# Moving small steps between the engines of a tuned attention and mixture-of-experts kernel: GpSimd scales one group, weights are asked for later, and the next attention's first scores sit inside the expert's output

## The chip, the cores and the metric

The kernel runs on one core of a Trainium2 chip. The metric is the device time in microseconds of one launch. Before the change it is 382.05 us, the median of three runs (381.8 to 382.43). The profile is of one such execution; its span, from the first to the last instruction, is 380.1 us.

The engines are named as in the profile: PE is the matrix engine (PEld its weight loads), DVE the vector engine, ACT the scalar engine, POOL is GpSimd, and SP the sync engine, which here only issues DMA transfers.

## The reference, cut to what matters

There are 8 batches of 384 tokens. Each batch goes through an attention with 16 query heads on 4 key and value heads, and the result, 384 x 1024, is the input x of a mixture of experts with 4 groups of 4 experts.

```python
# attention, per batch
scores = scale * np.matmul(q, k.transpose(0, 1, 3, 2))
attn = softmax(scores)
x = np.matmul(attn, v)                       # heads side by side: [B*S, 1024]
# mixture of experts, per token
g_idx = argmax(x @ w_group);  g_w = softmax weight of that group
e_idx = argmax(x @ w_expert[g_idx]);  e_w = softmax weight of that expert
h  = np.maximum(x @ w1[g, e], 0.0)
out = g_w * e_w * (h @ w2[g, e])
```

## The kernel before

An attention (`Attn`) runs in 24 units: 4 groups (one key head with its 4 query heads) of 6 key chunks. A unit makes scores on PE, takes exp on ACT into a tile `e` in SBUF, multiplies `e` with v on PE into the group's accumulator `oT` in PSUM, and lets POOL and DVE sum the `e` tiles for the softmax's denominator.

```python
def score(self, u):
    sT = ps_tile("s")                        # PSUM, two buffers in turn
    ... 4 matmuls ...                        # L305
    e = epool.tile([P, 2, S], F32, name="e") # 13 buffers
    nc.scalar.activation(e, sT, ACT.Exp, scale=scale)            # L311

def pv(self, u):
    if c == 0:
        self.oT[g] = ps_tile("o")            # PSUM, two buffers in turn
    ... 4 matmuls, oT[g] += v * e[u] ...     # L324

def tail(self, u):
    if c in (1, 3):
        self.add(nc.gpsimd, u - 1)           # L331: e[u-1] += e[u]
    if c >= 3:
        self.reduce(g, c - 3, ...)           # L338, DVE (can be held back)
    if c == NC - 1:
        self.reduce(g, NR - 1, z + 2)
        ...
        if b > 2 or (b == 2 and g > 1):
            nc.vector.tensor_copy(out=dst, in_=src)              # L371, oT -> xT
        else:
            nc.scalar.copy(out=dst, in_=src)                     # L373

def run(self, u0, u1, inserts, nxt=None):
    for u in range(u0, u1):
        if u + 2 < NU: self.score(u + 2)
        elif nxt is not None: nxt.score(u + 2 - NU)
        self.pv(u)
        self.tail(u)
        for f in inserts.get(u, []): f()     # other work, placed after unit u
```

`ps_tile("x")` gives the "o" buffer of PSUM that is not in turn; inserts use it. After the attention the sums of the denominators are gathered (`collect`, DVE), spread over partitions by a small matmul (`sums`, L405) and inverted (L409). For each pair of the eight column blocks (`m`), `spread` writes the inverses out with DVE transposes into `rb` (L416), `scale_x` multiplies `xT` by them (L425), and `cast` makes the bf16 copy `xb` that the expert reads.

The expert of a batch is guessed from the mean of v before its tokens are known, so that its weights can be fetched ahead; what a guess gets wrong is done in a loop at the end. `guess_mean` (L457) and `guess_logits` (L473) make the guess, `gate_logits` (L443) and `gate_tokens` (L468) the logits of the tokens, `gate_softmax` and `pick_index` are some 14 small DVE operations, and `pick`, `pick_w1` (L544) and `pick_w2` (L550) read the index on POOL and start the two weight transfers of 2048 KB each.

The first two batches are woven by hand:

```python
a = at[0]
a.run(0, NU, {
    ...
    9: [do(first_k, 1, "x", nc.vector)],
    10: [do(sums, 0, 0, 1, "x"), do(normalise, 0, 0)],
    13: [first_guess],
    15: [do(collect, 0, 1, 2), first_pick],
    16: [first_fetch],                       # pick, pick_w1(0)
    19: [do(sums, 0, 1, 2, "x")],
    20: [do(normalise, 0, 1)],
    21: [do(pick_w2, 0)],
}, at[1])
collect(0, 2, Hkv)
loads(2)                                     # v, k and q of batch 2
a = at[1]
hold(a)
a.run(0, FU, {                               # FU = 15
    2: [do(cast, 0, 0)],
    4: [do(cast, 0, 1)],
    7: [do(sums, 0, 2, Hkv, "x")],
    8: [do(normalise, 0, 2, "x"), do(normalise, 0, 3, "x"), a.release, do(transposes, 2)],
    11: [do(cast, 0, 2)],
    13: [do(cast, 0, 3)],
})
moe_h(0, 0, "s")                             # expert 0, first half (L606, L608)
...
a.run(FU, NU, {})
```

From batch 2 on every batch is the same block: an attention, then the expert of the batch before it. The end of the expert's output (`ffn_y`, L615) for its third chunk of tokens, and the start of the next attention:

```python
y = ffn_y(w2s[f], hTs[f], 2, "o", (0,))      # first half of the columns
guess_logits(vm, glp)
at[b + 1] = Attn(b + 1)
at[b + 1].score(0)
weights[b] = gate_softmax(b, glp, not last)
pick_index(b + 1)
ffn_y(w2s[f], hTs[f], 2, "o", (1,), y)       # second half
at[b + 1].score(1)
return {1: [do(y_out, f, 2, y, True)]}       # half on ACT, half on DVE, after unit 1
```

Of the kernel before, what the change touches and what calls it, by code (L numbers as in the profile page):

```python
# [9 lines left out]
F32 = mybir.dt.float32  # L10
# [3 lines left out]
ALU = mybir.AluOpType  # L14
# [4 lines left out]
def kernel(  # L19
# [218 lines left out]
    def evac(eng, out_, in_):  # L238
        if eng is nc.scalar:
            eng.copy(out=out_, in_=in_)  # L240
        else:
            eng.tensor_copy(out=out_, in_=in_)  # L242
# [46 lines left out]
    class Attn:  # L289
# [62 lines left out]
        def tail(self, u):  # L352
            b = self.b
            g, c = u // NC, u % NC
            z = u - c
            if c in (1, 3):
                self.add(nc.gpsimd, u - 1)
            if c >= 3:
                self.reduce(g, c - 3, (z, z + 4, z + 5)[c - 3])
            if c == NC - 1:  # L360
                self.reduce(g, NR - 1, z + 2)
                if b not in xT:
                    if b == 1:
                        w = wpool.tile([P, KQ, F], BF16, name="w1")
                        xT[b] = w.rearrange("p a f -> p (a f)").bitcast(F32)[
                            :, :KQ * S].rearrange("p (a n) -> p a n", n=S)
                    else:
                        xT[b] = xpool.tile([P, KQ, S], F32, name="xT", bufs=1)
                dst, src = xT[b][:, KG * g:KG * (g + 1), :], self.oT[g][:, :, :S]
                if b > 2 or (b == 2 and g > 1):  # L370
                    nc.vector.tensor_copy(out=dst, in_=src)  # L371
                else:
                    nc.scalar.copy(out=dst, in_=src)  # L373
# [37 lines left out]

    def spread(b, m, which=None):

        rb = gpool.tile([P, 2, S], F32, name="rb") if which is None else ps_tile(which)[:, :, :S]
# [12 lines left out]
    def normalise(b, m, which=None):  # L427
        scale_x(b, m, spread(b, m, which), nc.vector)

    def cast(b, m):  # L430
        ks = slice(2 * m, 2 * m + 2)
        nc.scalar.copy(out=xb[b][:, ks, :], in_=xT[b][:, ks, :])  # L432

# [13 lines left out]
        nc.scalar.copy(out=ls, in_=lg[:, :S])  # L447
        lgs[b] = ls

    def guess_mean(b, pt, eng=None):  # L450

        pm = pt[:, 1, :Hkv]
        v16 = vraw[b].rearrange("p h x -> p (h x)").bitcast(BF16)
        for g in range(Hkv):
            for i in range(SC):
                e0 = g * NC * D + i * P
                nc.tensor.matmul(out=pm[:, g:g + 1], lhsT=v16[:, 2 * e0 + 1:2 * (e0 + P):2],  # L457
                                 rhs=onesb[:, :1], start=(i == 0), stop=(i == SC - 1))
        vm = gpool.tile([P, Hkv], BF16, name="vm")
        evac(eng or nc.vector, vm, pm)  # L460
        return vm

    def gate_rows(pt):
# [146 lines left out]
    def ffn_y(w2, hT, c, which, nhs=(0, 1), y=None):  # L610
        if y is None:
            y = ps_tile(which)
        for nh in nhs:
            for f in range(FQ):
                nc.tensor.matmul(out=y[:, nh, :], lhsT=hT[:, f, c * P:(c + 1) * P],  # L615
                                 rhs=w2[:, f, nh * HALF:(nh + 1) * HALF],
                                 start=(f == 0), stop=(f == FQ - 1))
        return y

    hTs = {}  # L620

# [5 lines left out]
    def y_out(b, c, y, split=False):  # L627
        ot = opool.tile([P, DM], F32, name="ot")
        if split:
            nc.scalar.mul(ot[:, :HALF], y[:, 0, :], weff[b][:, c:c + 1])  # L630
            nc.vector.tensor_scalar(ot[:, HALF:], y[:, 1, :], weff[b][:, c:c + 1], None,  # L631
                                    op0=ALU.mult)
        else:
            nc.scalar.mul(ot, y.rearrange("p a n -> p (a n)"), weff[b][:, c:c + 1])  # L634
        for ps, x in halves(c):
            nc.sync.dma_start(out=out_rows(out[b * S:(b + 1) * S])[x], in_=ot[ps])

# [3 lines left out]
    def do(f, *a):  # L641
        return lambda: f(*a)
# [21 lines left out]

    def first_guess():
        state["pt"] = ps_tile("x")
        state["vm"] = guess_mean(0, state["pt"], nc.scalar)

    def first_pick():
        glp = gate_rows(state["pt"])  # L670
# [19 lines left out]
    def hold(a):  # L690
        a.held = []

    GB = KG * SC
    a = at[0]
    a.run(0, NU, {
# [2 lines left out]
        4: [gate_matrix_b],  # L698
        6: [do(collect, 0, 0, 1)],
        7: [do(first_q, 2 * GB, 2 * GB, "x", nc.vector)],  # L700
        9: [do(first_k, 1, "x", nc.vector)],
        10: [do(sums, 0, 0, 1, "x"), do(normalise, 0, 0)],
        13: [first_guess],
        15: [do(collect, 0, 1, 2), first_pick],
        16: [first_fetch],
        19: [do(sums, 0, 1, 2, "x")],
        20: [do(normalise, 0, 1)],
        21: [do(pick_w2, 0)],
    }, at[1])
    collect(0, 2, Hkv)  # L710
    loads(2)

    FU = 15
    a = at[1]
    hold(a)
    a.run(0, FU, {
        2: [do(cast, 0, 0)],
        4: [do(cast, 0, 1)],
        7: [do(sums, 0, 2, Hkv, "x")],
        8: [do(normalise, 0, 2, "x"), do(normalise, 0, 3, "x"), a.release, do(transposes, 2)],  # L720
        11: [do(cast, 0, 2)],
        13: [do(cast, 0, 3)],
    })
    moe_h(0, 0, "s")
    pt = ps_tile("x")
    gate_logits(0, pt)
    moe_h(0, 2, "s")
    glp = gate_rows(pt)
    gate_tokens(0, glp)
    vm = guess_mean(1, pt, nc.scalar)  # L730
    collect(1, 0, 2)
    sums(1, 0, 2, "s")
    for m in range(2):
        normalise(1, m)
    moe_h(0, 4, "s")
    guess_logits(vm, glp)
    weights[0] = gate_softmax(0, glp, True, nc.scalar)
# [5 lines left out]
    def first_block():  # L743

        prefetch(1)
        collect(1, 2, Hkv)
        weights[0]()
        out_weights(0)
        cast(1, 0)
        cast(1, 1)  # L750
        moe_y(0, 0, "s")
        y = ffn_y(w2s[0], hTs[0], 1, "s", (0,))
        sums(1, 2, Hkv, "o")
        normalise(1, 2)
        normalise(1, 3)
        ffn_y(w2s[0], hTs[0], 1, "s", (1,), y)
        y_out(0, 1, y)
        cast(1, 2)
        cast(1, 3)
        nc.sync.dma_start(out=xb_dram[1], in_=xb[1])  # L760
        y = ffn_y(w2s[0], hTs[0], 2, "o", (0,))
        at[2] = Attn(2)
        at[2].score(0)
        ffn_y(w2s[0], hTs[0], 2, "o", (1,), y)
        at[2].score(1)
        return {1: [do(y_out, 0, 2, y, True)], 3: [second_logits], 19: [second_gate],
                21: [second_pick]}

    def second_logits():
        gate_logits(1, ps_tile("x"))  # L770

    def second_gate():
        state["pt"] = ps_tile("x")
        gate_tokens(1, gate_rows(state["pt"]))
        state["vm"] = guess_mean(2, state["pt"])

    def second_pick():
        glp = gate_rows(state["pt"])
        guess_logits(state["vm"], glp)
        weights[1] = gate_softmax(1, glp, True, nc.scalar)  # L780
        pick_index(2)

    def prefetch(b):
# [8 lines left out]
    def block(b):  # L792
        last = b == B - 1
        f = b - 1
        prefetch(b)
        moe_h(f, 0, "s")
        collect(b, 0, Hkv)
        weights[f]()
        out_weights(f)
        moe_h(f, 2, "s")  # L800
        sums(b, 0, Hkv, "o")
        for m in range(4):
            normalise(b, m)
# [12 lines left out]
        pt = ps_tile("s")  # L816
        glp = gate_rows(pt)
        gate_tokens(b, glp)
        vm = None if last else guess_mean(b + 1, pt)
        y = ffn_y(w2s[f], hTs[f], 2, "o", (0,))  # L820
        if not last:
            guess_logits(vm, glp)
            at[b + 1] = Attn(b + 1)
            at[b + 1].score(0)
        weights[b] = gate_softmax(b, glp, not last)
        if not last:
            pick_index(b + 1)
        ffn_y(w2s[f], hTs[f], 2, "o", (1,), y)
        if not last:
            at[b + 1].score(1)  # L830
            return {1: [do(y_out, f, 2, y, True)]}
        y_out(f, 2, y, True)
        weights[b]()
        out_weights(b)

# [119 lines left out]
```

The softmax here doesn't subtract the row's maximum and nothing guards it: scores larger than these inputs give would overflow.

## Time and profile before

| | before |
|---|---|
| time, median of 3 | 382.05 us |
| span of the profiled execution | 380.1 us |
| PE busy | 364.6 us, 96% |
| DVE busy | 261.9 us, 69% |
| ACT busy | 232.6 us, 61% |
| POOL busy | 147.3 us, 39% |
| granted PE clock | 0.996 |

PE busy is the union of its matmuls' time, so what is left, 15.5 us, is the time in which no matmul was under way. The chain that ended last runs through PE for 78% of the span, DVE for 13% and ACT for 6%. Where it leaves PE, another engine kept PE waiting. These places lie in the first two attentions, at the start of the third, and for about four microseconds at the start of each later one.

### The profile page before, as it was taken

Reading aid. Unit: us, or ns where it says so; the run is one execution under the profiler, and the core shown is the slowest. Engines: PE = TensorE matmul, PEld = TensorE weight load, DVE = VectorE, ACT = ScalarE, POOL = GpSimd, SP = SyncE. Lnnn points to the kernel's source line nnn. Section 1 sums busy time; section 2 is a strip of 40 time slices with the busy share of each in tenths; the row PEclk is TensorE's granted clock in tenths of the full one; section 3 lists DMA queues with packets and bytes.
Section 4 is the critical chain, followed back from the end, with each engine's and each line's share of the span. In section 5 each row is a group of like instructions: output and inputs, shape, how many; then the busy total and the mean of one; then the engine's idle time right before and its main releaser. Section 6 shows DMA issues by size and latency. Waiting matters only on the chain.

```text
span 380.1 us, 8950 instructions
## 1 busy us (share of the span) xinstructions
PE 364.6 (96%) x3663; PEld 193.9 (51%) x3663; DVE 261.9 (69%) x494; ACT 232.6 (61%) x315; POOL 147.3 (39%) x116
## 2 busy tenths in 40 slices
PE   8999799999989999999999999999999999999992
PEld 3444356444545455545555455554555456554541
DVE  4789978847689279854998279883798449983130
ACT  4779945768824498256953489344982569544321
POOL 5657730716613077212653047330772036600000
PEclk9999999999999999999999999999999999999998
DMA  8975999999999999899999999999998999199734
GB/s 190 247 115 93 238 211 149 241 237 260 207 160 223 252 248 184 173 211 297 213 148 221 228 278 208 148 220 254 244 185 163 182 282 228 30 207 220 236 68 100
DMA packets 71209, 76.02 MB, mean 200 GB/s; under 512 B 35928, under 2 KB 50264, under 8 KB 71168
## 3 DMA queue, kind: packets, MB, share of 16 engines
q0 software_dynamic: 26640, 41.03, 61.8%
q1 hardware_dynamic: 44096, 33.81, 36.1%
q10 hardware_dynamic: 432, 0.61, 0.5%
q8 instruction: 29, 0.48, 0.5%
q14 instruction: 12, 0.10, 0.1%
HBM read 89.21 MB, written 18.87 MB: 284 GB/s over the span
## 4 chain that ended last, share of the span: by engine, by line
PE 78%; DVE 13%; ACT 6%; issue 2%; ACTq 0%; DVEq 0%; POOLq 0%
PE ps_o L324 22%; PE ps_s L606 18%; PE ps_s L615 14%; PE ps_o L615 7%; PE ps_s L305 7%; ACT e L311 4%; DVE red L338 4%; PE ps_o L443 3%; DVE xT L425 2%; DVE rb L416 2%; PE ps_o L268 1%; PE ps_o L606 1%; DVE w L425 1%; PE ps_s L468 1%; PE ps_o L405 1%
## 5 line engine op out<-in xcount | busy, mean ns | idle before, releaser
L331 POOL TENSOR_TENSOR e<-e 128x768 f32<-128x768 f32 x64 | 116.1, 1830 | 138.5 <-ACT e L311 91.5
L311 ACT ACTIVATE e<-ps_s 128x768 f32<-128x768 f32 x192 | 149.1, 819 | 25.2 <-PE ps_s L305 23.5
L324 PE MATMUL ps_o<-e,v_raw 64*64 64x384 f32 x1536 | 153.8, 482 | 1.6 <-DVE xT L425 1.6
L338 DVE TRANSPOSE_TENSOR_REDUCE red<-e 128x24 f32<-128x768 f32 x128 | 114.1, 946 | 10.5 <-POOL e L331 10.5
L606 PE MATMUL ps_s<-xb,w 128*128 128x384 bf16 x480 | 81.0, 326 | 0.0
L324 PEld LDWEIGHTS ps_o<-e,v_raw 64*64 64x64 f32 x1536 | 61.0, 133 | 28.5 <-issue 20.0
L305 PE MATMUL ps_s<-qT,kT 64*64 64x384 bf16 x768 | 67.1, 327 | 3.0 <-ACT e L311 1.7
L608 ACT ACTIVATE hT<-ps_s 128x768 bf16<-128x768 f32 x30 | 24.3, 811 | 70.9 <-PE ps_s L606 70.9
L606 PEld LDWEIGHTS <-w 128*128 128x128 bf16 x512 | 48.8, 98 | 36.3 <-issue 4.8
L615 PEld LDWEIGHTS <-hT 128*128 128x128 bf16 x384 | 36.0, 98 | 45.4 <-issue 5.4
L615 PE MATMUL ps_s<-w,hT 128*128 128x512 bf16 x248 | 56.4, 379 | 0.0
L305 PEld LDWEIGHTS <-kT 64*64 64x64 bf16 x768 | 29.4, 104 | 42.6 <-issue 39.1
L615 PE MATMUL ps_o<-w,hT 128*128 128x512 bf16 x136 | 32.0, 379 | 0.0
L416 DVE STREAM_TRANSPOSE rb<-inv 128x384 f32<-128x384 f32 x60 | 31.1, 557 | 1.0
L425 DVE TENSOR_TENSOR xT<-xT,rb 128x768 f32<-128x768 f32 x26 | 28.2, 1086 | 0.9
L634 ACT ACTIVATE ot<-ps_s,we 128x1024 f32<-128x1024 f32 x14 | 15.6, 1116 | 19.1 <-PE ps_s L615 19.1
L432 ACT CAST xb<-xT 128x768 bf16<-128x768 f32 x28 | 22.1, 832 | 0.0
L371 DVE COPY xT<-ps_o 128x768 f32<-128x768 f32 x22 | 20.2, 919 | 0.0
L242 DVE CAST vm<-ps_s 128x4 bf16<-128x4 f32 x5 | 0.8, 163 | 27.4 <-PE ps_s L457 27.4
L663 POOL COPY after<-qT 128x1 bf16<-128x1 bf16 x7 | 1.3, 189 | 40.5 <-DMA qT<-q_raw 37.5
L631 DVE TENSOR_SCALAR ot<-ps_o,we 128x512 f32<-128x512 f32 x7 | 5.3, 750 | 15.6 <-ACT ot L630 11.3
L409 DVE RECIPROCAL inv<-ps_o 128x96 f32<-128x96 f32 (+2 forms) x10 | 6.0, 603 | 7.0 <-PE ps_o L405 7.0
(129 smaller groups left out, 189.3 us busy)
## 6 DMA issues: line engine op xcount, KB each, us to landing
w<-in_moe_w_dram POOLq DMA_DIRECT2D x16, 2048.0 KB, 21.9
out_dram<-ot SPq DMA_DIRECT2D x42, 256.0 KB, 7.0
xb_scratch<-xb SPq DMA_DIRECT2D x8, 768.0 KB, 9.8
q_raw<-in_q_dram POOLq DMA_DIRECT2D x7, 768.0 KB, 33.6
v_raw<-in_v_dram SPq DMA_DIRECT2D x14, 384.0 KB, 7.3
out_dram<-ot SPq DMA_DIRECT2D x11, 128.0 KB, 2.3
k<-in_k_dram POOLq DMA_DIRECT2D x7, 192.0 KB, 30.3
w<-in_q_dram POOLq DMA_DIRECT2D x3, 192.0 KB, 7.3
```

The lines of the kernel that those rows point to most:

```text
L305: nc.tensor.matmul(out=sT[r * H2:(r + 1) * H2, s, :S], lhsT=kT[b][s * D:(s + 1) * D, slot, ks], rhs=qT[b][s * D:(s + 1) * D, kq * SC:(kq + ...
L311: nc.scalar.activation(e.rearrange("p t (s x) -> p s t x", s=2), sT[:, :, :S].rearrange("p s (t x) -> p s t x", t=2), ACT.Exp, scale=scale)
L324: nc.tensor.matmul(out=oT[t * D:(t + 1) * D, r, :S], lhsT=vraw[b][r * H2:(r + 1) * H2, g, c * D:(c + 1) * D], rhs=self.e[u][r * H2:(r + 1) ...
L331: eng.tensor_add(out=self.e[u], in0=self.e[u], in1=self.e[u + 1])
L338: nc.vector.tensor_reduce(out=reds[self.b][:, g, n].rearrange("p t j -> p (t j)"), in_=self.e[u].rearrange("p t (j x) -> p (t j) x", x=32) ...
L371: nc.vector.tensor_copy(out=dst, in_=src)
L416: nc.vector.transpose(out=rb[:, r].rearrange("p (j x) -> p j x", x=32), in_=inv[b][:, 2 * m + r].unsqueeze(2).to_broadcast([P, NB, 32]))
L425: eng.tensor_mul(out=x, in0=x, in1=rb)
L432: nc.scalar.copy(out=xb[b][:, ks, :], in_=xT[b][:, ks, :])
L606: nc.tensor.matmul(out=h[:, jj, :S], lhsT=w1[:, kq, (f0 + jj) * P:(f0 + jj + 1) * P], rhs=x[:, kq, :], start=(kq == 0), stop=(kq == KQ - 1))
L608: nc.scalar.activation(hT[:, f0:f0 + 2, :], h[:, :, :S], ACT.Relu)
L615: nc.tensor.matmul(out=y[:, nh, :], lhsT=hT[:, f, c * P:(c + 1) * P], rhs=w2[:, f, nh * HALF:(nh + 1) * HALF], start=(f == 0), stop=(f == ...
```

## The change

The change moves steps; the arithmetic stays, and nothing is left out.

- In the first attentions GpSimd takes over the multiplication and the bf16 copy of batch 0's group 1, and the multiplication of batch 1's first two groups; the copy of group 0 moves ahead into attention 0. Keys are transposed one unit earlier. The sums of batch 0's groups 2 and 3 come three units earlier, their normalisation two units earlier, and the held reductions are released three units later. This is to take work from DVE and ACT while both have more than PE.
- The second weights of expert 0 and the loads of batch 2 are asked for later, so that the first weights have the transfers to themselves; DVE takes the `xT` copies of batch 1's group 1 and of batch 2's first two groups.
- Batch 1's logits and its gate come out of attention 2's units 3, 19 and 21: the logits into the expert's output before it, the gate to unit 2.
- Both first scores of an attention sit inside the second half of the expert's last output chunk, three of whose eight steps come before them and five after, and the whole chunk is then written by DVE. This is to have the first two exps done by the time the attention begins.

The diff, cut:

```diff
-                if b > 2 or (b == 2 and g > 1):
+                if b > 1 or (b, g) == (1, 1):
                     nc.vector.tensor_copy(out=dst, in_=src)
...
-        rb = gpool.tile([P, 2, S], F32, name="rb") if which is None else ...
+        rb = gpool.tile([P, 2, S], F32, name="rb", bufs=2) if which is None else ...
...
-    def cast(b, m):
+    def cast(b, m, eng=None):
         ks = slice(2 * m, 2 * m + 2)
-        nc.scalar.copy(out=xb[b][:, ks, :], in_=xT[b][:, ks, :])
+        evac(eng or nc.scalar, xb[b][:, ks, :], xT[b][:, ks, :])
...
+    def y_scores(f, a, y):
+        ffn_y(w2s[f], hTs[f], 2, "o", (1,), y, range(FQ // 2 - 1))
+        a.start()                            # score(0), score(1)
+        ffn_y(w2s[f], hTs[f], 2, "o", (1,), y, range(FQ // 2 - 1, FQ))
+        y_out(f, 2, y, nc.vector)
...
+    def first_scale():
+        scale_x(0, 1, state["rb"], nc.gpsimd)
+        cast(0, 1, nc.gpsimd)
+    def first_spread():
+        state["rb"] = spread(0, 1)
...                                          # attention 0
-        9: [do(first_k, 1, "x", nc.vector)],
+        8: [do(first_k, 1, "x", nc.vector)],
...
+        14: [do(cast, 0, 0)],
...
-        20: [do(normalise, 0, 1)],
-        21: [do(pick_w2, 0)],
+        20: [first_spread],
+        21: [first_scale],
     }, at[1])
     collect(0, 2, Hkv)
-    loads(2)
...                                          # attention 1
-        2: [do(cast, 0, 0)],
-        4: [do(cast, 0, 1)],
-        7: [do(sums, 0, 2, Hkv, "x")],
-        8: [do(normalise, 0, 2, "x"), do(normalise, 0, 3, "x"), a.release, do(transposes, 2)],
-        11: [do(cast, 0, 2)],
+        3: [do(pick_w2, 0)],
+        4: [do(sums, 0, 2, Hkv, "x")],
+        6: [do(normalise, 0, 2, "x"), do(normalise, 0, 3, "x")],
+        9: [do(load_k, 2), do(load_q, 2)],
+        10: [do(cast, 0, 2)],
+        11: [a.release],
         13: [do(cast, 0, 3)],
     })
     moe_h(0, 0, "s")
+    load_v(2)
+    transposes(2)
...
     for m in range(2):
-        normalise(1, m)
+        scale_x(1, m, spread(1, m), nc.gpsimd)
...                                          # the expert's output before attention 2
         y = ffn_y(w2s[0], hTs[0], 2, "o", (0,))
+        gt = ps_tile("x")
+        guess_mean(2, gt)
+        gate_logits(1, gt)
+        state["vm"] = mean_copy(gt, nc.vector)
         at[2] = Attn(2)
-        at[2].score(0)
-        ffn_y(w2s[0], hTs[0], 2, "o", (1,), y)
-        at[2].score(1)
-        return {1: [do(y_out, 0, 2, y, True)], 3: [second_logits], 19: [second_gate],
-                21: [second_pick]}
+        y_scores(0, at[2], y)
+        return {2: [second_gate]}
...                                          # the later blocks
         if not last:
             guess_logits(vm, glp)
-            at[b + 1] = Attn(b + 1)
-            at[b + 1].score(0)
         weights[b] = gate_softmax(b, glp, not last)
         if not last:
             pick_index(b + 1)
+            at[b + 1] = Attn(b + 1)
+            y_scores(f, at[b + 1], y)
+            return {}
         ffn_y(w2s[f], hTs[f], 2, "o", (1,), y)
-        if not last:
-            at[b + 1].score(1)
-            return {1: [do(y_out, f, 2, y, True)]}
-        y_out(f, 2, y, True)
+        y_out(f, 2, y, nc.vector)
```

More of the change, by code (lines that the diff above doesn't have):

```diff
@@ L412, in spread @@
     def spread(b, m, which=None):
-        rb = gpool.tile([P, 2, S], F32, name="rb") if which is None else ps_tile(which)[:, :, :S]
+        rb = gpool.tile([P, 2, S], F32, name="rb", bufs=2) if which is None else ps_tile(which)[:, :, :S]
         for r in range(2):
@@ L448, in gate_logits, with guess_mean @@
         lgs[b] = ls
-    def guess_mean(b, pt, eng=None):
+    def guess_mean(b, pt):
         pm = pt[:, 1, :Hkv]
@@ L458, in guess_mean, with mean_copy @@
                                  rhs=onesb[:, :1], start=(i == 0), stop=(i == SC - 1))
+    def mean_copy(pt, eng):
         vm = gpool.tile([P, Hkv], BF16, name="vm")
-        evac(eng or nc.vector, vm, pm)
+        evac(eng, vm, pt[:, 1, :Hkv])
         return vm
@@ L608, in ffn_h, with ffn_y @@
         nc.scalar.activation(hT[:, f0:f0 + 2, :], h[:, :, :S], ACT.Relu)
-    def ffn_y(w2, hT, c, which, nhs=(0, 1), y=None):
+    def ffn_y(w2, hT, c, which, nhs=(0, 1), y=None, fs=None):
         if y is None:
@@ L613, in ffn_y @@
         for nh in nhs:
-            for f in range(FQ):
+            for f in (range(FQ) if fs is None else fs):
                 nc.tensor.matmul(out=y[:, nh, :], lhsT=hT[:, f, c * P:(c + 1) * P],
@@ L625, in moe_h, with y_out @@
         ffn_h(xb[b], w1s[b], hTs[b], f0, which)
-    def y_out(b, c, y, split=False):
+    def y_out(b, c, y, eng=None):
         ot = opool.tile([P, DM], F32, name="ot")
[L629 to L632, printed above, removed]
+        w = weff[b][:, c:c + 1]
+        if eng is None:
+            nc.scalar.mul(ot, y.rearrange("p a n -> p (a n)"), w)
         else:
-            nc.scalar.mul(ot, y.rearrange("p a n -> p (a n)"), weff[b][:, c:c + 1])
+            eng.tensor_scalar(ot, y.rearrange("p a n -> p (a n)"), w, None, op0=ALU.mult)
         for ps, x in halves(c):
@@ L666, in first_guess @@
         state["pt"] = ps_tile("x")
-        state["vm"] = guess_mean(0, state["pt"], nc.scalar)
+        guess_mean(0, state["pt"])
+        state["vm"] = mean_copy(state["pt"], nc.scalar)
     def first_pick():
@@ L729 @@
     gate_tokens(0, glp)
-    vm = guess_mean(1, pt, nc.scalar)
+    guess_mean(1, pt)
+    vm = mean_copy(pt, nc.scalar)
     collect(1, 0, 2)
@@ L751, in first_block @@
         moe_y(0, 0, "s")
-        y = ffn_y(w2s[0], hTs[0], 1, "s", (0,))
         sums(1, 2, Hkv, "o")
@@ L755, in first_block @@
         normalise(1, 3)
-        ffn_y(w2s[0], hTs[0], 1, "s", (1,), y)
-        y_out(0, 1, y)
+        moe_y(0, 1, "s")
         cast(1, 2)
@@ L761, in first_block @@
         y = ffn_y(w2s[0], hTs[0], 2, "o", (0,))
+        gt = ps_tile("x")
+        guess_mean(2, gt)
+        gate_logits(1, gt)
+        state["vm"] = mean_copy(gt, nc.vector)
         at[2] = Attn(2)
-        at[2].score(0)
-        ffn_y(w2s[0], hTs[0], 2, "o", (1,), y)
-        at[2].score(1)
-        return {1: [do(y_out, 0, 2, y, True)], 3: [second_logits], 19: [second_gate],
-                21: [second_pick]}
-    def second_logits():
-        gate_logits(1, ps_tile("x"))
-    def second_gate():
[L773 to L778, printed above, removed]
+        y_scores(0, at[2], y)
+        return {2: [second_gate]}
+    def second_gate():
+        glp = gate_rows(ps_tile("x"))
+        gate_tokens(1, glp)
         guess_logits(state["vm"], glp)
-        weights[1] = gate_softmax(1, glp, True, nc.scalar)
+        weights[1] = gate_softmax(1, glp, True)
         pick_index(2)
@@ L818, in block @@
         gate_tokens(b, glp)
-        vm = None if last else guess_mean(b + 1, pt)
+        if not last:
+            guess_mean(b + 1, pt)
+            vm = mean_copy(pt, nc.vector)
         y = ffn_y(w2s[f], hTs[f], 2, "o", (0,))
```

## The prediction

> **What bounds the kernel now.** I read the page first, then who PE waited for, then PE's timeline at those places, then the other engines there.
>
> ```profile
> PE 364.6 (96%) x3663; PEld 193.9 (51%) x3663; DVE 261.9 (69%) x494; ACT 232.6 (61%) x315; POOL 147.3 (39%) x116
> PE ps_s L305 <- ACT e L311: 1.7, 8, 0.3
> PE ps_o L324 <- DVE xT L425: 1.6, 1, 1.6
> PE ps_o L405 <- DVE smx L512: 1.3, 1, 1.3
> PE ps_s L305 <- DVE kT L242: 0.7, 1, 0.7
> PE ps_o L405 <- DVE rsum L397: 0.6, 1, 0.6
> ```
>
> PE is the bound: it idles 15.5 us. 1.6 us of that is the start and 6.8 us the drain in the last window (352 to 380.1 us: PE 21.27 of 28.10), both outside the change. About 7 us are left, and the waits name most of them (us in total, times, longest). The union hides short stops, as a matmul's record runs past the start of the next. So I count stops by starts: a unit of an attention (scores 0.16, PV 0.65 in the chain) takes 0.81 us, and what two starts lie further apart is lost.
>
> ```profile
> 45.52 0.33 PE L305 MATMUL ps_s<-qT,kT 64*64 64x384 bf16 x4
> 47.44 0.88 PE L324 MATMUL ps_o<-e,v_raw 64*64 64x384 f32 x8 [1.59 <-DVE xT L425]
> ...
> 132.37 0.82 PE L324 MATMUL ps_o<-e,v_raw 64*64 64x384 f32 x8
> 133.35 0.36 PE L305 MATMUL ps_s<-qT,kT 64*64 64x384 bf16 x4 [0.17 <-ACT e L311]
> ...
> 135.12 0.84 PE L324 MATMUL ps_o<-e,v_raw 64*64 64x384 f32 x8
> 136.03 0.36 PE L305 MATMUL ps_s<-qT,kT 64*64 64x384 bf16 x4
> ```
>
> First pair: 1.92 us between starts 0.16 apart by work, 1.76 lost. Second and third: 0.98 and 0.91 where 0.65 is work, 0.33 + 0.26 lost, about 0.56 with the next starts taken in; this repeats every 44.2 us. Three sums:
> - **A**, 8 to 50 us (attention 0, 15 units of attention 1): 0.75 at 20.46, 0.22 at 35.38, 0.42 at 38.22, 0.52 at 40.35, 0.76 at 41.92, 1.76 at 47.44: **4.4 us**.
> - **B**, attention 2 and the expert behind it: 0.49 at 82.80, 0.28 at 91.24, 0.30 at 96.39, 0.6 at 101.95, 1.38 at 113.08: **3.05 us**.
> - **C**, the starts of attentions 3 to 7: 5 x 0.56: **2.8 us**.
>
> So about 10.2 us can be had at most.
>
> ```profile
> 30.00:50.00 20.00, 17.24 (x249) 8.74 (x246) 19.02 (x23) 19.18 (x27) 15.84 (x12) 1.00 0.93 183
> ...
> 32.16 3.61 POOL L331 TENSOR_TENSOR e<-e 128x768 f32<-128x768 f32 x2
> 33.53 4.26 DVE L425 TENSOR_TENSOR xT<-xT,rb 128x768 f32<-128x768 f32 x1
> ```
>
> The window's busy columns are PE, PEld, DVE, ACT, POOL. In A, DVE (19.02 of 20) and ACT (19.18) are full. One DVE product took 4.26 us, where the row's fastest take 0.96, while POOL ran two adds and three DMA issues.
>
> [...] the products at 44.19 and 46.44 us, whose `rb` lies in PSUM, take 0.95 beside POOL's adds. [...] weights in a block land 20 us after issue, the last block's first, with less beside it, after 13.5.
>
> **The change part by part.**
>
> *A.* Keys one unit earlier: the transposes end near 18.9 and the DVE copy (0.56) near 19.6, before the score that needs them at 19.8. Saves 0.7. Group 1's product on POOL frees DVE of 4.26 us; DVE gains the copy of batch 1's group 1 (0.92). The last four reductions of attention 0 then end near 37 instead of 41.3, `rsum` near 37.4, and the sums, now after unit 4, reach PE near 37.2: 0.3 lost for 0.76. The inverse ends near 38.5, but the spread's PSUM buffer is free only when ACT has copied group 0, near 39.6; two spreads and two products (4.4 us, from the 42.94 to 47.39 us of before) end at 44.1. PV of unit 12 needs that buffer near 43.8: 0.3 lost for 1.76. ACT: units 24 to 38 carry 15 exps x 0.74 (five took 3.71 at 135.14), one `xT` copy and two casts, 0.75 each, 13.4 us, against 15.6 before (two copies, four casts) and about 12.5 of PE's. The cast moved into attention 0 (0.73) uses the slack there. I let ACT lose 0.5 in all. Left over 1.1 of 4.4: **saves 3.3**, so the expert starts near 46.6 instead of 49.9.
>
> *Weights.* `w1` of expert 0 is issued at 31.22 and lands 17.1 later, at 48.3: too late for 46.6. Without v of batch 2 (issued at 33.8) and w2 beside it I take 13.5 to 14.5: 45 to 46. The later w2 must wait on POOL for two old adds (3.6), the product (1.83), the cast (about 1.0, from 0.50 for half the size) and two adds (3.6): issued near 42 and, landing 22.6 us after issue as before at most, there by 64, with PE needing it at 67.5. q and k of batch 2 go out near 47 and land near 60 (before 63), as they follow the same bytes. **Cost 0.**
>
> *Batch 1 on POOL.* Two products, 3.7 us, near 56 to 60, give DVE 1.9 us and let the index come earlier. PE waits for none of it. **0.**
>
> *B.* Batch 1's last sums come after one output chunk instead of one and a half, so xT is scaled by about 75.6 and the logits (1.43) find it at 77. The 1.43 + 0.9 + 0.1 of gate work on PE only move. The start of attention 2 loses nothing: 0.5 saved. Then DVE gets 1.36 (whole output chunk), about 3.65 of gate operations (105.30 to 108.78 before) and two copies (1.84) inside the 20 us of the attention. Its own 16 reductions and four copies are 16 x 0.89 + 4 x 0.92 = 17.9. DVE is 3 to 5 us behind, more if POOL's adds stop its two-input gate operations. The reductions of group 0 start near 87 to 89 and its copy ends near 92 to 94; PV of unit 12 wants the buffer near 91.3. New stall 0.5 to 2.9, taken as 1.4. The old four (2.56) go, as DVE is no later relative to PE at the sums. **Saves 0.5 + 1.2.**
>
> *C.* From the second half's start T: three steps (3 x 0.216), scores by T + 1.1, exps end near T + 1.9 and T + 2.65, five more steps end near T + 2.3. Score 2 needs the first exp, unit 1 (T + 3.1) the second: no stop. ACT is rid of 0.70 here, then makes an exp in 0.74 to PE's 0.81. DVE is done with the index at T + 3.6 and the chunk (1.36) at T + 5.0; its first reduction before was at T + 5.7. **Saves 0.5 x 5 = 2.5.**
>
> Sum: 3.3 + 0.5 + 1.2 + 2.5 = 7.5, so 374.5; with 0.3 for a stop I don't see, **374.8 us**.
>
> **The rivals.**
> 1. *The transfers take over.* From block to block POOL waits about 7 us for the transposed q before it may ask for weights, and that loop repeats every 44.2 us by itself. PE's block falls to 43.7. But in a block weights issued at 115.36 land near 135.4 and are used at 152.05, and the queries that POOL sees at 159.26 are used at 174.16: 15 us and more to spare, so even 8 us earlier PE meets them. Only a late w1 of expert 0 could cost 1 to 3 us. Then 376 to 377.
> 2. *DVE becomes the bound in attention 2.* For it: 23 us of work in 20. If POOL's adds block several gate operations (one took 0.54 instead of 0.17 at 105.51), the stall at unit 12 is 3 or more and B gains nothing: 376.5.
> 3. *ACT keeps A bound.* ACT holds 19.18 of 20 now. If only half its stops go, A saves 2: 376.
> 4. *All goes well:* 1.1 left in A is 0.3 and B's stall nil: 372.
>
> **Range and chances.** Two rivals together give 378.4; a sum without new stalls 372. The line of 2% is 374.4, just under my number; a larger gain needs nearly every step to hold. Slower than before by over 2% would need a new wait of over 15 us, and I see no queue that long. Faster 0.42, same 0.56, slower 0.02.
>
> **What would show it.** PE's busy time stays near 364.6 and idle falls to 8 or 9. The first expert matmul (L606) starts at 46 to 47.5. No PE wait on xT L425 above 0.5, none on kT. PV of attention 2's unit 12 shows a wait on DVE's copy. The blocks from attention 3 on repeat every 43.7. No PE wait names a DMA. A wait on w1 at 46, or a stop of over 3 us in attention 2, would prove me wrong, as would a block of 44.2.

## The result and the profile after

The changed kernel takes **379.22 us** (median of four runs, 377.87 to 379.66), against 382.01 us for the kernel before on the same chip: a ratio of 0.992, 95% interval 0.9893 to 0.9946. The prediction was 374.8 us, with a range that ended at 378.4. So about 3 us came of an expected 7. The profiled span is 377.9 us, against 380.1.

From the page and the list of whom PE waited for (us in total, times, longest), of the kernel after:

```profile
PE 363.3 (96%) x3663; PEld 184.1 (49%) x3663; DVE 266.8 (71%) x495; ACT 228.0 (60%) x303; POOL 154.8 (41%) x120
...
PE ps_o L324 <- DVE xT L371: 2.4, 1, 2.4
PE ps_o L405 <- DVE rsum L397: 2.4, 2, 2.1
...
PE ps_s L608 <- DMA w<-in_moe_w_dram: 0.6, 1, 0.6
PE ps_o L324 <- DVE xT L425: 0.2, 1, 0.2
```

The waits that the change was aimed at are gone (kT, ACT's e) or nearly so (1.6 us on xT is 0.2), and three others stand in their place: attention 2's unit 12 waits 2.4 us for DVE's copy, the sums of batch 1's last groups wait 2.1 us for DVE, and the first expert waits 0.6 us for its weights. Idle PE is 14.6 us instead of the 8 to 9 expected.

Where a gain is made and lost shows best when one milestone of PE after another is laid side by side. The loss all falls between 69 and 108 us:

| PE reaches | before | after | difference |
|---|---|---|---|
| first matmul of expert 0 | 49.87 | 47.70 | -2.2 |
| first output of expert 0 | 70.83 | 68.69 | -2.1 |
| start of its third output chunk | 78.21 | 78.25 | 0.0 |
| first matmul of expert 1 | 106.39 | 108.48 | +2.1 |
| guess of the next expert, in expert 1's output | 129.72 | 130.42 | +0.7 |
| last output of the last expert | 371.38 | 369.06 | -2.3 |

**The small gate operations.** PE's 2.1 us before the sums of batch 1 lead to DVE, and there to the 14 operations of batch 0's gate. DVE's timeline after (start, duration, operation), four of its lines, the first three in a row:

```profile
59.73 1.36 DVE L488 TENSOR_TENSOR sh<-gl,mx 128x16 f32<-128x16 f32 x1
61.13 1.74 DVE L492 TENSOR_SCALAR ohg<-sh 128x16 f32<-128x16 f32 x1
62.90 0.23 DVE L494 TENSOR_TENSOR pr<-gl,ohg 128x64 f32<-128x64 f32 x1
...
65.03 1.74 DVE L569 SCALAR_TENSOR_TENSOR t<-eidx,oh_all 128x16 f32<-128x16 f32 x1
```

And POOL's in the same stretch:

```profile
57.48 3.58 POOL L425 TENSOR_TENSOR w<-w,rb 128x768 f32<-128x768 f32 x2 [8.01 <-DVE rb L416]
61.02 1.81 POOL L331 TENSOR_TENSOR e<-e 128x768 f32<-128x768 f32 x1
64.92 3.75 POOL L331 TENSOR_TENSOR e<-e 128x768 f32<-128x768 f32 x2 [2.09 <-PE ps_s L305]
```

Read the ends. POOL's two products, new in this change, end at 57.48 + 3.58 = 61.06; DVE's L488 started under them and ends at 61.09. POOL's next add ends at 62.83; L492, started 0.11 us into it, ends at 62.87. L494, four times as large and with POOL free, takes 0.23. L569 ends with the first of POOL's next two adds in the same way. So these operations, once started under a POOL instruction, end with that instruction. The chain took 7.4 us; the same chain with POOL out of the way takes 3.1 (below).

**Attention 2.** The same happens to batch 1's gate at unit 2: L488 takes 0.83 us, L569 1.68, and the chain runs from 87.69 to 93.24. The reductions and the copy queue behind it on DVE. Four of DVE's lines:

```profile
87.96 0.17 DVE L486 TENSOR_REDUCE mx<-gl 128x4 f32<-128x16 f32 x1
88.17 0.83 DVE L488 TENSOR_TENSOR sh<-gl,mx 128x16 f32<-128x16 f32 x1
...
91.37 1.68 DVE L569 SCALAR_TENSOR_TENSOR t<-eidx,oh_all 128x16 f32<-128x16 f32 x1
...
96.64 0.92 DVE L371 COPY xT<-ps_o 128x768 f32<-128x768 f32 x1
```

POOL's adds run from 85.36 to 88.96 here. L488 is held by them until 89.00, but the reduction L486, which reads just as many elements, starts under them too and takes 0.17 us. So it is not every small operation that is held: the traces show it for those with two tensors as input (L488, L562 and L569, 0.81 to 1.75 us) and for TENSOR_SCALAR (L492 and L566, 1.55 to 1.75 us), which take 0.17 to 0.23 us otherwise. PE's timeline after at unit 12:

```profile
94.87 0.33 PE L305 MATMUL ps_s<-qT,kT 64*64 64x384 bf16 x4
97.61 1.56 PE L324 MATMUL ps_o<-e,v_raw 64*64 64x384 f32 x8 [2.40 <-DVE xT L371]
...
99.26 1.50 PE L324 MATMUL ps_o<-e,v_raw 64*64 64x384 f32 x8
```

Starts that should lie 0.16 us apart lie 2.74 apart: 2.6 lost. And then the PV matmuls take 1.56 and 1.50 us instead of 0.81. PE's windows there (window and its length; PE busy, PEld, DVE, ACT, POOL, each with its number of instructions; then PEclk, the granted clock, and two columns on DMA) say why:

```profile
96.00:98.00 2.00, 0.39 (x4) 0.30 (x8) 2.00 (x3) 0.12 (x1) 0.00 (x0) 0.82 1.12 212
98.00:100.00 2.00, 2.00 (x20) 0.79 (x16) 2.00 (x3) 0.47 (x1) 0.67 (x1) 0.50 1.12 213
100.00:102.00 2.00, 2.00 (x32) 0.95 (x28) 2.00 (x4) 1.33 (x3) 1.33 (x2) 0.82 1.14 206
```

From the end of the stop on the clock is granted at half for some 3.4 us (97.30 to 100.71), which costs another 1.5. PE counts as busy in that time, so no list of waits names it.

**The later blocks.** PE's timeline after at the start of attention 3:

```profile
131.26 0.52 PE L305 MATMUL ps_s<-qT,kT 64*64 64x384 bf16 x8
131.71 1.25 PE L617 MATMUL ps_o<-w,hT 128*128 128x512 bf16 x5
132.89 0.36 PE L305 MATMUL ps_s<-qT,kT 64*64 64x384 bf16 x4
133.08 0.81 PE L324 MATMUL ps_o<-e,v_raw 64*64 64x384 f32 x8
```

Both first scores, five steps of the expert, then the units at 0.81 us with no stop; the blocks repeat every 43.6 us instead of 44.2.

### The profile page after: what moved, and what is told of

Read it like the earlier page. It is cut to its first block, busy times and chain, and to the rows that moved or that the text cites. A ratio compares the mean times of both kernels' runs of the same rounds, so it can differ in the third digit from the quotient of the medians.

```text
span 377.9 us, 8930 instructions
## 1 busy us (share of the span) xinstructions
PE 363.3 (96%) x3663; PEld 184.1 (49%) x3663; DVE 266.8 (71%) x495; ACT 228.0 (60%) x303; POOL 154.8 (41%) x120
## 4 chain that ended last, share of the span: by engine, by line
PE 86%; DVE 6%; DMA 4%; issue 1%; ACT 0%
PE ps_o L324 27%; PE ps_s L608 20%; PE ps_s L617 13%; PE ps_o L617 8%; PE ps_s L305 8%; DMA w<-in_moe_w_dram 4%; PE ps_o L443 3%; DVE red L338 3%; PE ps_o L268 1%; PE ps_o L608 1%; PE ps_s L470 1%; PE ps_o L405 1%; DVE sh L488 1%; DVE ohg L492 1%; PE ps_s L457 0%
## 5 line engine op out<-in xcount | busy, mean ns | idle before, releaser
L324 PEld LDWEIGHTS ps_o<-e,v_raw 64*64 64x64 f32 x1536 | 55.8, 134 | 40.1 <-issue 25.9
L305 PE MATMUL ps_s<-qT,kT 64*64 64x384 bf16 x768 | 64.0, 328 | 0.3
L305 PEld LDWEIGHTS <-kT 64*64 64x64 bf16 x768 | 24.7, 105 | 38.8 <-issue 37.0
L671 POOL COPY after<-qT 128x1 bf16<-128x1 bf16 x7 | 2.6, 378 | 56.0 <-DMA qT<-q_raw 53.1
L425 DVE TENSOR_TENSOR xT<-xT,rb 128x768 f32<-128x768 f32 x25 | 24.0, 959 | 0.9
L371 DVE COPY xT<-ps_o 128x768 f32<-128x768 f32 x24 | 22.0, 919 | 0.0
L240 ACT CAST xb<-xT 128x768 bf16<-128x768 f32 x27 | 21.1, 827 | 0.0
L242 DVE COPY gl<-ps_s 128x80 f32<-128x80 f32 (+1 forms) x6 | 1.4, 238 | 14.0 <-PE ps_s L475 8.4
L642 DVE TENSOR_SCALAR ot<-ps_o,we 128x1024 f32<-128x1024 f32 x7 | 9.0, 1284 | 2.9 <-PE ps_o L617 2.9
```

The source lines that it names most:

```text
L305: nc.tensor.matmul(out=sT[r * H2:(r + 1) * H2, s, :S], lhsT=kT[b][s * D:(s + 1) * D, slot, ks], rhs=qT[b][s * D:(s + 1) * D, kq * SC:(kq + ...
L324: nc.tensor.matmul(out=oT[t * D:(t + 1) * D, r, :S], lhsT=vraw[b][r * H2:(r + 1) * H2, g, c * D:(c + 1) * D], rhs=self.e[u][r * H2:(r + 1) ...
L425: eng.tensor_mul(out=x, in0=x, in1=rb)
```

## The experiments

The theory was: the gate's operations on DVE are held by POOL; PE's two stops of over 2 us follow from that; the half clock follows from such a stop. The rivals: DVE simply has too much work there, and the slow clock comes from the load and lands anywhere. Diffs are against the changed kernel unless it says otherwise. The kernel before took 382.0 to 383.0 us in these comparisons, so ratios, not times, are to be compared; 0.001 is 0.38 us.

### The parts alone

**Only the first part** (kernel before, with attentions 0 and 1 up to the first expert as after):

```diff
+    def first_scale():
+        scale_x(0, 1, state["rb"], nc.gpsimd)
+        cast(0, 1, nc.gpsimd)
...                                          # and the other inserts of both, as after
     moe_h(0, 0, "s")
+    load_v(2)
+    transposes(2)
```

> The kernel before with the change's first part alone: attentions 0 and 1 up to the first expert, with POOL's product and copy for group 1 of batch 0, the later weights and the later reductions. All behind it is as before. Theory: the first expert matmul starts near 47.7 instead of 49.9 and the 2.2 us stay, as the rest of the old kernel has no wait that takes them back: 0.993 to 0.9955 of the kernel before. Rival: the old sums of batch 1 and attention 2 take half of it back; then 0.997.

Measured: 380.06 us, ratio 0.993 (0.9914 to 0.9947), 2.7 us gained. PE waits 0.8 us for w1 here too; all behind the first expert's first half is as before.

**Only the last part** (kernel before, with both scores inside the expert's output from the second block on):

```diff
+        ffn_y(w2s[f], hTs[f], 2, "o", (1,), y, range(FQ // 2 - 1))
+        a.start()
+        ffn_y(w2s[f], hTs[f], 2, "o", (1,), y, range(FQ // 2 - 1, FQ))
+        y_out(f, 2, y, eng=nc.vector)
```

> The kernel before with one part of the change: from batch 2 on, both first scores sit inside the second half of the expert's last output chunk and DVE writes the whole chunk. Attentions 0, 1 and 2 are as before. Theory: each of the five starts of attentions 3 to 7 gains 0.5 to 0.6 us and nothing comes back, so 379.0 to 379.5, and the blocks repeat every 43.6 us. Rival: part of the gain of the later blocks in the changed kernel comes from what the early parts leave them (earlier transfers); then 380.5 to 381.5.

Measured: 379.66 us, ratio 0.9921 (0.9896 to 0.9947), 3.0 us gained. The two parts alone bring 2.7 + 3.0 = 5.7 us, the whole change about 3.1: what lies between, the gate and the sums up to attention 2, **costs** some 2.6 us. The milestones above give 2.9.

### Who holds the gate

**Batch 1's two products back on DVE:**

```diff
-        scale_x(1, m, spread(1, m), nc.gpsimd)
+        normalise(1, m)
```

> The changed kernel with batch 1's first two products back on DVE; nothing else differs. Theory: the two products on POOL, and the add they push behind them, block DVE's small gate operations (three of them took 1.4 to 1.7 us instead of 0.2), so the last sums of batch 1 come 2.1 us late. Then no gate operation of batch 0 takes over 0.5 us, the PE wait on rsum near 74 us falls from 2.1 to under 0.5 us although DVE has 1.9 us more to do, and the time falls by 1.5 to 2.5 us, to 377. Rival: the sums wait because they were moved ahead of the second output chunk and DVE can't be ready by then; then the wait stays near 2 us or grows to 4, and the time is 379 to 381.

Measured: 377.95 us, ratio 0.9867 (0.9822 to 0.9912), some 2 us below the change; the intervals overlap a little, so the trace has to decide. DVE's timeline in this version:

```profile
60.60 0.17 DVE L492 TENSOR_SCALAR ohg<-sh 128x16 f32<-128x16 f32 x1
...
62.93 0.18 DVE L569 SCALAR_TENSOR_TENSOR t<-eidx,oh_all 128x16 f32<-128x16 f32 x1
```

No operation of the gate takes over 0.27 us, the chain 3.1. DVE has 1.9 us more work and is done 3.7 us earlier. The wait of 2.1 us at batch 1's sums is gone; PE's line there names none:

```profile
72.20 0.42 PE L405 MATMUL ps_o<-rsum,half 128*64 128x24 f32 x8
```

Taking work off DVE had made it later. The stop at unit 12 (2.39) and the slow clock behind it (0.50 from 98 to 100 us) stay, so that stop has a cause of its own.

**Batch 1's gate at unit 19, as before:**

```diff
-        return {2: [second_gate]}
+        return {19: [second_gate]}
```

> The changed kernel with batch 1's gate moved from unit 2 of attention 2 to unit 19; nothing else differs. Theory: at unit 2 the gate's small DVE operations stand ahead of all reductions and copies of attention 2, so that the PSUM buffer for unit 12 comes free 2.6 us late, and the clock that drops after that idle time costs another 1.5 us. Then the PE wait on the copy (L371, 2.40 us) goes, the granted clock is back at 0.995 or more in every run, and the time falls from 379.2 to 375.5 to 376.5. Rival: DVE simply has 23 us of work in 20 us in attention 2 (two more copies, a whole output chunk), wherever the gate stands; then the wait stays above 1.5 us or moves to the sums at the end of attention 2, and the time is 378 to 379.

Measured: 378.31 us, ratio 0.9882 (0.9838 to 0.9926). No wait at unit 12 and no slow clock in the trace (1.00 from 95 to 105 us); but PE now loses 0.9 us at 102.74, where the gate's rows wait for DVE's copy (0.6 at the same place before), and 1.27 at the next sums (113.28). The stop of 2.11 us at batch 1's sums stays as well. The gate's place decides who waits, and moving it back mostly trades: the expected 375.5 to 376.5 us did not come. By the intervals this run is not told from the change itself.

**Four POOL additions of attention 2 left out** (the sums of batch 2's first two groups lack those terms):

```diff
-            if c in (1, 3):
+            if c in (1, 3) and not (b == 2 and g < 2):
                 self.add(nc.gpsimd, u - 1)
```

> The changed kernel, with the four pair additions of attention 2's first two head groups left out on GpSimd (two for each group), and nothing put in their place: the sums of batch 2's first two groups lack those terms, the count of TensorE instructions is the same. Theory (the gate is late because GpSimd's additions hold VectorE): the two gate operations that took 0.83 and 1.68 us beside them take 0.17 to 0.3 us, the gate's chain takes 3 to 3.7 us instead of 5.5, the wait for the copy at unit 12 falls from 2.4 us to about 0.5, no slow clock follows it, and the time falls by 2 to 3.5 us, to 376 to 377. Rival (VectorE's plain load in these 12 units, the gate, the reductions and two copies, is the cause): the gate's operations may be quicker or not, but the wait at unit 12 stays above 1.5 us and the time moves by under 1 us.

Measured: 375.74 us, ratio 0.9838 (0.9797 to 0.9878), a gain of about 3.1 us over the change (0.992 less 0.9838), though DVE and PE do the same work. DVE's timeline of this version:

```profile
88.20 0.17 DVE L488 TENSOR_TENSOR sh<-gl,mx 128x16 f32<-128x16 f32 x1
...
90.74 0.18 DVE L569 SCALAR_TENSOR_TENSOR t<-eidx,oh_all 128x16 f32<-128x16 f32 x1
...
94.50 0.92 DVE L371 COPY xT<-ps_o 128x768 f32<-128x768 f32 x1
```

The copy starts at 94.50 instead of 96.64: the 2.1 us are just what L488 and L569 lost before (0.66 + 1.50). The wait at unit 12 is 0.2 us, and no slow clock follows (1.00 from 95 to 105 us). DVE's plain load is the same, so it isn't the cause of the 2.4 us.

### What sets off the slow clock

**Eleven matmuls of ones behind attention 2's unit 11** (their result is not read):

```diff
+    def second_fill():
+        t = ps_tile("s")
+        for i in range(11):
+            nc.tensor.matmul(out=t[:, i % 2, :], lhsT=onesb[:, :P], rhs=onesb, start=True, stop=True)
-        return {2: [second_gate]}
+        return {2: [second_gate], 11: [second_fill]}
```

> The changed kernel with eleven matmuls of ones (128 x 512, 0.216 us each, their result is never read) put on PE after unit 11 of attention 2, where PE otherwise stands still for about 2.5 us; nothing else differs. Theory: the granted clock falls to half for some 3 us because PE stood still, and that costs 1.5 us. Then the PV of unit 12 still starts when the copy is done, but at full speed, the clock is 0.995 or more in every run unless the 2.1 us stop at 74 us sets it off instead, and the time falls by 1.2 to 1.5 us. Rival: the clock falls whatever PE does there; then the time is the same or up to 0.5 us longer.

Measured: 379.15 us, ratio 0.9905 (0.9885 to 0.9925). The slow clock at unit 12 is gone, but in the trace it now follows the other stop, the 2.11 us at 74.46, where the change itself had none: the output chunk behind it takes 5.24 us instead of 3.63. So the expected 1.2 to 1.5 us did not come.

**The same with batch 1's products on DVE:**

```diff
-        scale_x(1, m, spread(1, m), nc.gpsimd)
+        normalise(1, m)
...                                          # and the eleven matmuls as above
```

> The changed kernel with batch 1's two products on VectorE and 11 matmuls of ones, whose result nothing reads, behind unit 11 of attention 2. With the products alone (377.95 us) one stop of TensorE of over 2 us was left, at unit 12, and the clock was granted at half for about 3 us behind it; with the matmuls alone that went away, and a slow stretch followed the stop at 74 us. Theory (a stop of 2 us or more sets off the slow clock, and nothing else does): no such stop is left, so the mean clock is 0.995 or more in all runs, and the time is 1 to 1.8 us below that of the products alone, at 376.2 to 377, although TensorE does the same work and 11 matmuls more. Rival (the slow stretch comes from the load over the whole execution and lands anywhere): the mean clock stays at 0.990 to 0.993 in most runs, and the time is within 0.5 us of 377.95.

Measured: 375.62 us, ratio 0.9819 (0.9798 to 0.9841). The clock is 0.995 to 0.997 in all four runs. PE's timeline:

```profile
92.24 2.55 PE L791 MATMUL ps_s<-onesb 128*128 128x512 bf16 x11
94.72 0.36 PE L305 MATMUL ps_s<-qT,kT 64*64 64x384 bf16 x4
94.91 0.83 PE L324 MATMUL ps_o<-e,v_raw 64*64 64x384 f32 x8
```

The filler takes as long (2.55 us) as the wait that it covers, so it gains nothing by itself; still the ratio is 0.0048 below that of the products alone, some 1.8 us. (The two intervals, 0.9822 to 0.9912 and 0.9798 to 0.9841, overlap a little; the clocks, 0.990 to 0.995 against 0.995 to 0.997, do so only at their ends, and the one run of the products alone with a clock of 0.995 took 375.61, like the runs here.) With PE kept busy over this wait the clock stayed full (1.00 from 92 to 104 us).

### The weights

**v of batch 2 asked for behind the transposes:**

```diff
-    load_v(2)
     transposes(2)
+    load_v(2)
```

> The changed kernel with the load of batch 2's v behind the transposes of batch 2 in the sync engine's order; nothing else differs. Theory: that load still starts at 33.2 us in the changed kernel, beside the first weights, and makes them land at 47.7. Then the first weights land 13.5 to 14.5 us after their issue at 30.8, the first expert matmul starts at 47.0 with no wait on a transfer, and the time falls by 0.7 us, to 378.5. Rival: the weights' own rate sets their landing; then it stays at 17 us after issue and the time at 379.2.

Measured: 379.82 us, ratio 0.9929 (0.9906 to 0.9951). The wait on w1 is gone: issued at 31.37, it is there when the first expert starts at 47.58, so it landed within 16.2 us of its issue instead of 16.9. The expert starts then although everything before it ran 0.6 us later than in the trace of the change, from the first scores on (7.50 instead of 6.92). The time didn't follow: in the trace the later start takes up what the wait gave, the slow clock costs as much as in the change, and the intervals don't tell the two apart. PE's timeline:

```profile
74.32 0.42 PE L405 MATMUL ps_o<-rsum,half 128*64 128x24 f32 x8 [2.12 <-DVE rsum L397]
74.67 5.31 PE L617 MATMUL ps_s<-w,hT 128*128 128x512 bf16 x16
```

Behind this stop the output chunk takes 5.31 us instead of 3.63, while behind the later stop at 99.16, of 2.39 us, the clock stays full (1.00 from 97 to 103 us).

### Towards a better version

**Batch 1's gate right behind attention 2's first scores**, inside the expert's output:

```diff
         a.start()
+        if mid is not None:
+            mid()                 # second_gate, its rows in the logits' own PSUM tile
         ffn_y(w2s[f], hTs[f], 2, "o", (1,), y, range(FQ // 2 - 1, FQ))
...
-        return {2: [second_gate]}
+        return {}
```

> The changed kernel with batch 1's gate moved from unit 2 of attention 2 into the expert's last output half, right behind the two first scores; nothing else differs. Theory: what hurts is that the gate's small DVE operations stand ahead of the reductions and are held up twice by POOL's adds (1.68 and 0.83 us for operations of 0.2). Three units earlier they start near 84 instead of 87.7 us; the reductions start near 88 to 90 instead of 93.2, PE waits under 1 us for the copy (L371), the clock doesn't drop, and the time is 0.981 to 0.985 of the kernel before. Rival: POOL's first two adds of attention 2 fall on the gate here as well, the reductions still start after 91.5, and the wait on the copy stays above 1.5 us; then 0.988 to 0.992.

Measured: 376.65 us, ratio 0.9838 (0.9821 to 0.9854). No wait at unit 12. The chain still meets POOL's additions (L562 takes 1.70 us, L566 1.55), and the output chunk's product behind it keeps unit 6 waiting 1.3 us.

**This, the products on DVE and the later v together:**

```diff
+    transposes(2)
     load_v(2)
-    transposes(2)
...
-        scale_x(1, m, spread(1, m), nc.gpsimd)
+        normalise(1, m)
...                                          # and mid(), as above
```

> The changed kernel with three mends at once: batch 1's products on DVE, batch 2's v loaded behind its transposes, and batch 1's gate inside the expert's output. Theory: the losses are separate and add up (2.1 us at the sums, 0.7 us at the first weights, 2.6 us and 1.5 us of slow clock in attention 2), so PE idles under 10 us in all, every run shows a clock of 0.996 or more, and the time is 0.974 to 0.979 of the kernel before, 372.5 to 374.5. Rival: what is gained early is lost at the next wait, as when attention 2 starts earlier and meets the same DVE; then 0.983 or more.

Measured: 374.5 us, ratio 0.9789 (0.9749 to 0.9828). Behind the start-up the waits that are left are 1.3 us at unit 6 and 0.5 in two others, and no slow clock shows (the mean is 0.994). PE idles 10.8 us, a little over the 10 expected. Two groups of DVE's operations in attention 2 (busy us, mean ns):

```profile
L562 DVE SCALAR_TENSOR_TENSOR key<-oh_all,eback 128x16 f32<-128x16 bf16 x1 | 1.7, 1690 | 0.0
L566 DVE TENSOR_SCALAR oh_all<-key,km 128x16 f32<-128x16 f32 x1 | 1.6, 1552 | 0.0
```

**And attention 2's first two additions on DVE** (against the version before):

```diff
-                self.add(nc.gpsimd, u - 1)
+                self.add(nc.vector if (b, g) == (2, 0) else nc.gpsimd, u - 1)
```

> The three edits together (batch 1's gate behind the first scores of attention 2, its two products on VectorE, the load of v behind the transposes), and the two pair additions of attention 2's first head group on VectorE in place of GpSimd. In the version with the three edits two small gate operations of VectorE took 1.69 and 1.55 us beside these additions, and the product of weights matrix 1's last output chunk stood behind them, which TensorE then waited 1.3 us for. Theory (VectorE is held by GpSimd's additions): every gate operation of 128x16 elements falls to 0.3 us or less, the output chunk's product is done some 3 us earlier, the wait of 1.3 us is gone, and the time falls by about 1.3 us to a ratio of 0.975 to 0.977 of the kernel before. Rival (VectorE has too much work there anyway, and the 1.9 us of additions put on it take the place of what was held): the gate gets faster but another wait of over 1 us on VectorE comes up at unit 12, and the time stays within 0.5 us of the three edits' (0.979).

Measured: 373.25 us, ratio **0.9772** (0.9726 to 0.9818), faster than both kernels. The same groups, with the additions that DVE has taken over:

```profile
L331 DVE TENSOR_TENSOR e<-e 128x768 f32<-128x768 f32 x2 | 1.8, 949 | 0.0
...
L566 DVE TENSOR_SCALAR oh_all<-key,km 128x16 f32<-128x16 f32 x1 | 0.2, 235 | 0.0
...
L562 DVE SCALAR_TENSOR_TENSOR key<-oh_all,eback 128x16 f32<-128x16 bf16 x1 | 0.2, 175 | 0.0
```

DVE took 1.8 us of work, at 0.95 us an addition against POOL's 1.83, and lost 2.8 us of blocking. The wait at unit 6 is gone, and the profiled span fell from 372.6 to 371.3 us, the expected 1.3. The ratios of the last two versions are too close for their intervals to tell them apart.

## Why the prediction was wrong, point by point

- **Batch 1 on POOL ("PE waits for none of it. 0."): the step that failed first.** I counted the 1.9 us that DVE is spared, and not that the two POOL products, with the adds that they push back, lie over DVE's gate. The chain took 7.4 us instead of 3.1, and PE stopped 2.1 us at batch 1's sums. Putting the products back took that stop away. The text had DVE's product of 4.26 us beside POOL's adds, but looked for such blocking only in large products; and of the two products that it names as running beside POOL's adds, only the one at 44.19 does: the adds end at 45.38, before the one at 46.44.
- **B ("saves 0.5 + 1.2", measured some 2.9 lost).** The mechanism of the stall at unit 12 was in the text, and so was "more if POOL's adds stop its two-input gate operations"; I put it in the rival at 3 us or more and in the sum at 1.4. It was 2.6, of which 2.2 is POOL's blocking: without the additions 0.2 was left as a wait. With the 2.1 us at the sums and 1.5 of slow clock, that makes 6.2 us lost where 3.05 were lost before: 3.15 more, and the milestones say 2.9.
- **The slow clock: not in the sum at all.** The only term that it could fall under is the 0.3 for "a stop I don't see"; it cost 1.5, and no list of waits shows it. The one of the change's four runs with a mean clock of 0.997 took 377.87 us, the three at 0.990 to 0.992 took 379.05 to 379.66.
- **Weights ("Cost 0"): wrong by 0.7.** w1 was issued at 30.78 and landed at 47.66, 16.9 us later, not 13.5 to 14.5. I had taken v of batch 2 to be out of its way; but SP had nothing ahead of v to wait for and issued it at 33.24, about as before, so it ran beside w1. A later line in the program was no later in time. With v behind the transposes w1 landed within 16.2 us, which was soon enough, and the wait was gone; whether it takes the 13.5 to 14.5 that the prediction had for a w1 without v beside it was not shown. The prediction named a wait on w1 as a thing that would prove it wrong.
- **A ("saves 3.3", measured 2.2).** Of the 4.4 us of stops 1.5 are left instead of 1.1, and w1 adds 0.7. The 0.4 are three small ones: a new 0.18 ahead of the keys' transposes, which now come a unit earlier (18.65), 0.47 instead of 0.3 at the sums (37.73), and 0.37 instead of 0.3 at unit 12 (44.58). What was left to ACT held: 0.22 and 0.28 for 0.5.
- **C ("saves 2.5", measured 3.0): right**, only 0.6 a block instead of 0.5. Alone it gives the same 3.0. "The transfers take over" didn't come true from block to block.

Of the rivals, the late w1 came true, and the stall of DVE in attention 2 in part: it was 2.6 us, not "3 or more", and by POOL's blocking, not by "23 us of work in 20". No rival had the stop at batch 1's sums or the slow clock. The text gave "two rivals together" 378.4; with these two on top the time went past it.

The blocking goes further than the "two-input gate operations" that the prediction had in mind: with one tensor as input, the TENSOR_SCALAR L492 took 1.74 us under POOL's add in the changed kernel, and L566 1.55 in the version with three edits, instead of 0.17 and 0.23.

## What to carry to other kernels

A chain of small DVE operations is priced by what POOL runs beside it: its operations with two tensors as input, and TENSOR_SCALAR, may wait for the end of a whole POOL instruction (up to 1.75 us for one of 0.2 here), so moving 1.9 us of work from DVE to POOL can make DVE 3.7 us later. Lay the two timelines over each other before giving POOL work, and keep long POOL operations away from chains on which PE waits. Price a PE stop of over 2 us at its length and at the risk of 1.5 us more (four of nine here), and ask of each transfer that is moved in the program what will hold it back in time.

## What was not expected of the hardware

**The clock after a stop.** In the traces of the change and its variants PE stops nine times for 2.1 to 2.4 us. After four of these the granted clock falls to 0.50, each time for 3.4 us (97.30 to 100.71 in the change), at a cost of 1.5 to 1.7; after five it stays full. The shorter stops of 1.59 us (at 47.44) and 1.32 us (at 113.08) in the kernel before, and the one of 1.27 us (at 113.28) with the gate at unit 19, are followed by the full clock.

| version | PE stops | us | clock |
|---|---|---|---|
| the change | 72.32 to 74.44 | 2.12 | full |
| the change | 95.20 to 97.61 | 2.40 | half from 97.30 |
| products on DVE | 92.97 to 95.36 | 2.39 | half from about 96.8 |
| gate at unit 19 | 73.70 to 75.81 | 2.11 | full |
| v later | 72.20 to 74.32 | 2.12 | half from about 74.7 |
| v later | 96.77 to 99.16 | 2.39 | full |
| gate behind the scores | 72.97 to 75.08 | 2.11 | full |
| eleven matmuls alone | 72.35 to 74.46 | 2.11 | half from about 74.7 |
| additions left out | 72.37 to 74.48 | 2.11 | full |

The length of the stop doesn't tell the two outcomes apart: 2.12 us was followed by the half clock with v later and by the full clock in the change, 2.39 us by the half clock with the products on DVE and by the full clock with v later. Nor does the half clock begin at a fixed distance from the stop: in the change it begins 0.3 us before the stop's end, with v later and with the eleven matmuls alone 0.3 to 0.4 us after it, and with the products on DVE some 1.4 us after it. The clock falls once more at the end of an execution, when PE has no work left: at 373.78 in the change, 2.8 us after its last matmul, and at 377.11 in the kernel before, 3.8 us after it. What decides whether a stop of over 2 us sets off the half clock was not shown, and no run was made to test it.
